# Planner of a fused attention, expert and MLP kernel: other lags, costs and engines in the plan, and the first expert's early rows split piece by piece

## The chip, the cores and the metric

One core of one Trainium2 chip. The time is that of one execution on the device in microseconds (us), the median of several runs. The engines are TensorE (PE in the rows, its weight loads PEld), VectorE (DVE), ScalarE (ACT), GpSimd (POOL) and SyncE (SP, which only starts transfers). They run side by side and wait for each other by semaphores.

## The reference, cut to what matters

```python
# q, k, v, alpha: [B=4, H=8, S=768, D=48]
for t in range(S):                                   # gated linear attention
    state = alpha[:, :, t, :, None] * state + einsum('bhd,bhe->bhde', k[:, :, t], v[:, :, t])
    y[:, :, t] = einsum('bhd,bhde->bhe', q[:, :, t], state)
x = y.transpose(0, 2, 1, 3).reshape(3072, 384)
logits = x @ w_gate                                  # [3072, 8]
expert_idx = argmax(logits, axis=1)                  # one expert for each token
gate_w = softmax(logits)[arange(N), expert_idx]
for e in range(8):                                   # w1: [8, 384, 1024], w2: [8, 1024, 384]
    xe = x[expert_idx == e]
    out[expert_idx == e] = gate_w[expert_idx == e, None] * (maximum(xe @ w1[e], 0) @ w2[e])
h = out @ w_in                                       # [3072, 384] @ [384, 2048]
return (h * (1 / (1 + exp(-1.702 * h)))) @ w_out     # @ [2048, 384]
```

## The kernel before, in words

**Attention.** The 3072 tokens are 24 tiles of 128 (`n` = 0 to 23; 4 batches of 6 chunks). For every group `g` of tiles VectorE forms running products of alpha by scans, forward (`Pf`, op `pf`) and backward (`Q`, op `qs`), and scales q with `Pf` (op `q`) and k with `Q` (op `k`). A scan of a group is cut into pieces of at most 386 columns; its second operand is a pattern of zeros and ones, `pat`. Op `k` runs on POOL for the groups in `MULT` (line 59), else on VectorE.

For each tile TensorE then forms scores (op `A`, into `atp`), ACT evicts them (`ats`), POOL masks them (an affine select), TensorE transposes k (op `K`, `ktp`), forms the product of k and v (`KV`, `kv`), the values (`X`, `xp` from `ats` and v) and the part from the state (`Y`, `xp` from q and `S`). The new state is the product plus the old state (op `SK`, an add on VectorE; for tiles with n < `ONTO`, line 60, TensorE adds the old state by a product with the identity instead) scaled on ACT. ACT evicts `x`, and TensorE forms `xtp` (op `T`), which holds the tile turned back and the eight logits.

**Routing**, for pairs of tiles (i = 0 to 11; 2i and 2i+1). VectorE: logits `lg`, their maximum, `d`, `sc`, `mx`, the one-hot choice `oh_all` (op `ch`, line 653) and running counts `cnt` (op `cn`). ACT: exponentials `ex`, their sum `gt` (VectorE inverts it) and the weighed rows `xw`, in four buffers, so that a pair's weighing needs the scatters of the pair two before. TensorE: op `B`, the rank (lines 683 to 688), three products that add into one PSUM tile:

```python
pe.matmul(ranks, ones, segr, start=True, stop=False)
pe.matmul(ranks, tri, oh_all[:, n0:n0 + 12, :], start=False, stop=False)
state["rk"] = pe.matmul(ranks, ones, cnt[:, n0:n0 + 12, :], start=False, stop=True)
```

VectorE makes row numbers `slots` of the ranks (op `so`), and POOL scatters the rows by them to `xs` in DRAM, sorted by expert (op `sc`, an indirect DMA). The ranks lie in the same PSUM tile as the scans' pattern (lines 379 to 381):

```python
bank = ps_1.tile([P, 512], F32, tag="lg", name="bank")
pat = bank[:, 0:HS]
ranks = bank[:, HS:HS + 12 * E].rearrange("p (n e) -> p n e", e=E)
```

**The plan.** All of this is handed to `Plan` (line 76) as ops: engine, cost in us, ops that it needs, a due time. `run` (line 124) simulates it 16 times: `passed` places, on the engine that can start first, the op with the smallest key among those that can start within `PATIENCE` of the earliest; an op is ready `HOP` after the ops that it needs; ops in `ALONE` on VectorE and POOL never overlap. Keys are due times first, then the latest starts of a pass backward from the end (the time after each op is the `tail` table), in the last 8 rounds with noise from `SEED`. The best order is then issued, and each engine keeps it. All these instructions carry line 73 (75 after).

**The end of the phase.** When 18 tiles are scattered, SP loads the first 224 rows of the first expert (op `early`, line 770). Behind T23, TensorE transposes them in three pieces of 128 columns each (op `te`, `turn_early`), and op `tx` splits them into a high and a low half, `xe_0` on ACT and `xe_1` on VectorE (`halve_early`). The first expert's first layer on these rows follows (line 331, `hp_0e` to `hp_7e`; ACT makes `he` of each), its second layer is line 348. On POOL pads follow the last scatters (line 812). Then the other rows, seven more experts (line 1005) and the second MLP.

Of the kernel before, what the change touches and what calls it, by code (L numbers as in the profile page):

```python
# [75 lines left out]
class Plan:  # L76
# [49 lines left out]
    def run(self, free, tail, rounds):  # L126
# [5 lines left out]
        self.apart = [name.rstrip("0123456789.") in ALONE.get(o[0], ()) for name, o in self.all.items()]  # L132
# [6 lines left out]
        rest = [tail.get(name, tail.get(name.rstrip("0123456789."), tail[""])) for name in names]  # L139
        hop = [HOP[e] for e in self.engine]  # L140
        rnd = random.Random(SEED)
        best = None
        for spread in (0.0, SPREAD):
            key = [o[3] for o in ops]
            for _ in range(rounds):
                start, order = self.passed(key, before, behind, lambda i, o: hop[i], ready, free)
# [11 lines left out]
def gla_moe_kernel(ctx: ExitStack, tc: tile.TileContext, hA, hkq, qT, kT, aT, qU, kU, aU, a0, v, wg, w1, w2, w_in, w_out, wgf, out):  # L158
# [198 lines left out]
    with ExitStack() as att:  # L357
# [196 lines left out]
        def step(n, got, pnds):
# [161 lines left out]
        for t, when in [("a.0", 4.1), ("k.0", 6.3), ("wg", 13.0)] + [(f"{t}.{c}", 7.0 + 3.2 * (c - 1) + w) for c in range(1, NC) for t, w in (("a", 0.6), ("k", 2.2))] + [(f"v{c}", 10.0 + 3.2 * c) for c in range(NC - 1)]:  # L716
# [665 lines left out]
```

## Time and profile before

| | us |
|---|---|
| median of 3 runs | 805.05 (804.11 to 806.07) |
| the profiled execution, by the clock of the runs | 804.12 |
| its span in the profile | 802.3 |
| mean granted clock of TensorE | 0.988 |
| attention and routing, up to the early rows' transposes | 0 to 143.6 |
| first expert's first product | 149.8 |
| experts and second MLP, TensorE busy throughout | to 790 |

The span is that of the records of one execution; the other 1.8 us lie around it. Times in rows are us from the span's start. A record's duration reaches a little into the next one's where instructions are pipelined. The bracket behind a row is the idle time of the engine before it and what ended it, as inferred from semaphores: with several semaphores the one that came last by the profile.

### The profile page before, as it was taken

Reading aid. Unit: us, or ns where it says so; the run is one execution under the profiler, and the core shown is the slowest. Engines: PE = TensorE matmul, PEld = TensorE weight load, DVE = VectorE, ACT = ScalarE, POOL = GpSimd, SP = SyncE. Lnnn points to the kernel's source line nnn. Section 1 sums busy time; section 2 is a strip of 40 time slices with the busy share of each in tenths; the row PEclk is TensorE's granted clock in tenths of the full one; section 3 lists DMA queues with packets and bytes.
Section 4 is the critical chain, followed back from the end, with each engine's and each line's share of the span. In section 5 each row is a group of like instructions: output and inputs, shape, how many; then the busy total and the mean of one; then the engine's idle time right before and its main releaser. Section 6 shows DMA issues by size and latency. Waiting matters only on the chain. (4 is left out here: it accounts for less than half of the span.)

```text
span 802.3 us, 13866 instructions
## 1 busy us (share of the span) xinstructions
PE 775.7 (97%) x5172; PEld 704.0 (88%) x5172; DVE 477.1 (59%) x913; ACT 382.4 (48%) x802; POOL 340.3 (42%) x435
## 2 busy tenths in 40 slices
PE   7998999799999999999999999999999999999995
PEld 5887778798889999999999989999999999999994
DVE  8988795569675657744588677754344443333331
ACT  5777787345463454445454455443333333223221
POOL 6663554509576658742366486550320303001001
PEclk9999999899999999999999999999999999999998
DMA  9998333357645564652134243220311303001001
GB/s 321 246 275 239 110 120 120 118 206 251 209 134 171 197 194 137 210 165 79 41 93 151 65 140 112 99 93 1 40 22 19 40 0 40 1 1 40 0 1 42
DMA packets 31836, 91.10 MB, mean 114 GB/s; under 512 B 6083, under 2 KB 11027, under 8 KB 31763
## 3 DMA queue, kind: packets, MB, share of 16 engines
q1 hardware_dynamic: 17584, 55.45, 22.7%
q0 software_dynamic: 11408, 30.98, 13.2%
q10 hardware_dynamic: 2771, 3.74, 1.5%
q8 instruction: 42, 0.69, 0.4%
q14 instruction: 31, 0.25, 0.1%
HBM read 70.87 MB, written 19.27 MB: 112 GB/s over the span
## 5 line engine op out<-in xcount | busy, mean ns | idle before, releaser
L1103 POOL DMA_INDIRECT out_y<-ob,perm x40 | 48.8, 1219 | 227.1 <-DVE ob L1099 216.9
L1069 DVE TENSOR_TENSOR h<-h,sg 128x512 f32<-128x512 f32 x96 | 66.9, 696 | 112.4 <-ACT sg L1068 112.1
L1088 PE MATMUL o<-whi,gh 128*128 128x384 f32 x384 | 130.1, 339 | 1.1 <-ACT gh L1072 1.1
L1088 PE MATMUL o<-wlo,gh 128*128 128x384 f32 x384 | 129.2, 337 | 0.0
L1088 PE MATMUL o<-whi,gl 128*128 128x384 f32 x384 | 126.2, 338 | 0.1
L1068 ACT ACTIVATE sg<-h 128x512 f32<-128x512 f32 x96 | 57.1, 595 | 118.5 <-PE h L1063 118.4
L1063 PE MATMUL h<-xh,wlo 128*128 128x512 f32 x288 | 113.2, 393 | 0.0
L1063 PE MATMUL h<-xh,whi 128*128 128x512 f32 x288 | 113.0, 392 | 0.0
L1063 PE MATMUL h<-xl,whi 128*128 128x512 f32 x288 | 112.6, 393 | 0.0
L1073 DVE TENSOR_TENSOR gl<-h,gh 128x512 fp32r<-128x512 f32 x96 | 66.3, 691 | 54.4 <-ACT gh L1072 52.7
L1072 ACT ACTIVATE gh<-h 128x512 fp32r<-128x512 f32 x96 | 57.4, 598 | 67.4 <-DVE h L1069 67.2
L1088 PEld LDWEIGHTS o<-whi,gh 128*128 128x128 f32 x384 | 72.1, 188 | 5.9 <-ACT gh L1072 1.9
L1088 PEld LDWEIGHTS o<-wlo,gh 128*128 128x128 f32 x384 | 72.1, 188 | 4.0
L1088 PEld LDWEIGHTS o<-whi,gl 128*128 128x128 f32 x384 | 71.8, 188 | 0.4 <-DVE gl L1073 0.4
L307 POOL TENSOR_TENSOR wlo<-stg,whi 128x512 fp32r<-128x512 f32 x42 | 57.6, 1398 | 18.8 <-ACT whi L299 18.7
L348 PE MATMUL yp<-hh,whi 128*128 128x224 f32 (+7 forms) x192 | 65.3, 343 | 0.2 <-ACT hh L333 0.2
L348 PE MATMUL yp<-hh,wlo 128*128 128x224 f32 (+7 forms) x192 | 64.9, 343 | 0.0
L1063 PEld LDWEIGHTS h<-xl,whi 128*128 128x128 f32 x288 | 54.1, 188 | 12.2
L348 PE MATMUL yp<-hl,whi 128*128 128x224 f32 (+7 forms) x192 | 63.2, 344 | 0.0
L1063 PEld LDWEIGHTS h<-xh,whi 128*128 128x128 f32 x288 | 54.2, 188 | 8.5
L1063 PEld LDWEIGHTS h<-xh,wlo 128*128 128x128 f32 x288 | 54.1, 188 | 8.4
L336 DVE SCALAR_TENSOR_TENSOR hl<-hp,hh 128x224 fp32r<-128x224 f32 (+7 forms) x64 | 34.8, 556 | 35.0 <-ACT hh L333 34.8
(269 smaller groups left out, 1574.6 us busy)
## 6 DMA issues: line engine op xcount, KB each, us to landing
stg<-in_w SPq DMA_DIRECT2D x30, 768.0 KB, 4.6
v<-in_v SPq DMA_DIRECT2D x24, 256.0 KB, 4.7
wf<-cvl POOLq DMA_DIRECT2D x48, 128.0 KB, 2.8
raw<-in_w_out POOLq DMA_DIRECT2D x24, 256.0 KB, 3.1
stg_m<-wf SPq DMA_DIRECT2D x8, 768.0 KB, 4.2
raw<-in_w_in POOLq DMA_DIRECT2D x18, 256.0 KB, 3.1
AB<-in_aU SPq DMA_DIRECT2D x24, 145.1 KB, 4.8
k<-in_kU SPq DMA_DIRECT2D x24, 144.0 KB, 4.6
```

Source lines behind the costliest of these rows:

```text
L307: POOL.tensor_sub(out=lo[:, cs], in0=st[:, cs], in1=hi[:, cs].bitcast(F32))
L336: DVE.scalar_tensor_tensor(out=h[1][:, f, :], in0=h_ps, scalar=0.0, in1=h[0][:, f, :].bitcast(F32), op0=ALU.max, op1=ALU.subtract)
L348: last["mm"] = PE.matmul(y_ps, w[:, c0:c0 + P], a[:, f, :], start=(i == 0), stop=(i == 23))
L1063: mm = PE.matmul(h_ps, w[:, c0:c0 + P], a[:, kk, :], start=(i == 0), stop=(i == 8))
L1068: ACT.activation(sg, h_ps, AF.Sigmoid, scale=QS)
L1069: DVE.tensor_mul(out=h_ps, in0=h_ps, in1=sg)
L1072: ACT.activation(gh, h_ps, AF.Copy)
L1073: DVE.tensor_sub(out=gl, in0=h_ps, in1=gh.bitcast(F32))
L1088: mm = PE.matmul(os[pt][t], a[:, ts], w[:, c0:c0 + DM], start=(f == f0 and first), stop=(f == f1 - 1 and a is gl))
L1103: POOL.indirect_dma_start(out=out_views[jj], out_offset=bass.IndirectOffsetOnAxis(ap=perm[:, jj:jj + 1], axis=0), in_=o_sb, in_offset=None ...
```

## The change

Costs in the plan are set nearer to what instructions take. A lag can now be set for a pair of ops: 2.5 us more from a scatter to what waits for it (a weighing, or the load of the early rows), 3.0 more from a pair's count to its rank, and 0.3 more into each op of TensorE from another engine. `PATIENCE`, `SEED`, the tail table and the load times are others. Four k products (groups 2, 7, 8 and 9) go from POOL to VectorE and two (10 and 16) from VectorE to POOL; the state of tile 4 is added on VectorE instead of TensorE. `te` and `tx` are cut into three ops each by 128 columns, with the low half (`tl`) an op of its own.

```diff
-MULT = (0, 1, 2, 3, 4, 5, 6, 7, 8, 9, 12)
-ONTO = 6
-SEED, SPREAD = 635, 0.6
-PATIENCE = {"PE": 0.03, "DVE": 0.05, "ACT": 0.3, "POOL": 0.3, "SP": 0.05}
+MULT = (0, 1, 3, 4, 5, 6, 10, 12, 16)
+ONTO = 4
+SEED, SPREAD = 582, 0.6
+PATIENCE = {"PE": 0.0, "DVE": 0.0, "ACT": 0.1, "POOL": 0.1, "SP": 0.1}
 ALONE = {"DVE": ("q", "k", "wl", "cn"), "POOL": ("s", "k", "pnd")}
+EXTRA = {("sc", "xw"): 2.5, ("sc", "early"): 2.5, ("cn", "B"): 3.0}
+EASE = 0.3
...
-        rest = [tail.get(name, tail.get(name.rstrip("0123456789."), tail[""])) for name in names]
-        hop = [HOP[e] for e in self.engine]
+        rest = [tail.get(name, tail.get(k, tail[""])) for name, k in zip(names, kind)]
+        lag = lambda i, o: HOP[self.engine[i]] + EXTRA.get((kind[i], kind[o]), EASE if self.engine[o] == "PE" != self.engine[i] else 0.0)
...
-                start, order = self.passed(key, before, behind, lambda i, o: hop[i], ready, free)
+                start, order = self.passed(key, before, behind, lag, ready, free)
...
-                late, _ = self.passed([-start[i] - self.cost[i] for i in every], behind, before, lambda i, o: hop[o], rest, dict.fromkeys(free, 0.0))
+                late, _ = self.passed([-start[i] - self.cost[i] for i in every], behind, before, lambda i, o: lag(o, i), rest, dict.fromkeys(free, 0.0))
...
-                    add(name, "POOL", 0.1 + 2.3 * f * part, [f"qs{g}", k_in], due - 0.6, lambda r=r: pool.tensor_mul(out=k[:, r], in0=ki[:, r], in1=it["Q"][:, r]))
+                    add(name, "POOL", 0.05 + 1.65 * f * part, [f"qs{g}", k_in], due - 0.6, lambda r=r: pool.tensor_mul(out=k[:, r], in0=ki[:, r], in1=it["Q"][:, r]))
...
-            add(f"q{g}", "DVE", 0.05 + 0.83 * f, [prev, q_in] + (ks if g == 0 else []), due, lambda: dve.tensor_mul(out=q, in0=qi, in1=it["Pf"][:, :, 0:CH]))
+            add(f"q{g}", "DVE", 0.05 + 0.83 * f, [prev, q_in], due, lambda: dve.tensor_mul(out=q, in0=qi, in1=it["Pf"][:, :, 0:CH]))
...
-            add(f"B{i}", "PE", 0.3, [f"cn{i}", f"so{i - 1}"], due + 14.5, rank)
+            add(f"B{i}", "PE", 0.28, [f"cn{i}", f"so{i - 1}"], due + 14.5, rank)
...
-                add(f"sc{n0 + j}", "POOL", 1.25, [f"so{i}", f"xw{n0 + j}"], due + 10 + 0.1 * j, lambda j=j: scatter(j))
...
+                add(f"sc{n0 + j}", "POOL", 1.1, [f"so{i}", f"xw{n0 + j}"], due + 10 + 0.1 * j, lambda j=j: scatter(j))
...
-        def turn_early():
-            xe.extend([ap.tile([P, KD, EARLY], F32R, name=f"xe_{i}") for i in range(2)])
-            for kk in range(KD):
-                turn_x0(pe, xe, 0, EARLY // GT, kk, ("kt", "kv", "at")[kk])
-
-        def halve_early():
-            for kk in range(KD):
-                halve_x0(act, dve, xe, 0, EARLY // GT, kk)
+        def turn_early(kk):
+            if kk == 0:
+                xe.extend(ap.tile([P, KD, EARLY], F32R, name=f"xe_{i}") for i in range(2))
+            turn_x0(pe, xe, 0, EARLY // GT, kk, ("kt", "kv", "at")[kk])
+
+        def high_early(kk):
+            last["x0"] = act.activation(xe[0][:, kk, :], state["t0", 0, kk], AF.Copy)
+
+        def low_early(kk):
+            last["lo"] = dve.tensor_sub(out=xe[1][:, kk, :], in0=state["t0", 0, kk], in1=xe[0][:, kk, :].bitcast(F32))
 
         plan.need("wh3", f"x{NT - 1}")
         plan.need("wl3", "unused")
-        add("te", "PE", 2.4, ["early", f"T{NT - 1}"], BEGIN + PITCH * (NT + 1), turn_early)
-        add("tx", "ACT", 1.1, ["te"], BEGIN + PITCH * (NT + 2), halve_early)
-        plan.run({"DVE": 4.0, "ACT": 4.0, "POOL": 5.3, "PE": 6.3, "SP": 14.0}, {f"T{NT - 1}": 29.0, f"sc{NT - 1}": 25.0, "wl2": 25.0, "wl3": 21.0, "jk": 0.0, "qm": 0.0, "": 19.0}, 8)
+        free = ["early", f"T{NT - 1}", f"KV{NT - 2}", f"x{NT - 1}"]
+        for kk in range(KD):
+            add(f"te{kk}", "PE", 0.8, free, BEGIN + PITCH * (NT + 1) + kk, lambda kk=kk: turn_early(kk))
+            add(f"tx{kk}", "ACT", 0.33, [f"te{kk}"], BEGIN + PITCH * (NT + 1) + kk, lambda kk=kk: high_early(kk))
+            add(f"tl{kk}", "DVE", 0.33, [f"tx{kk}"], BEGIN + PITCH * (NT + 1) + kk, lambda kk=kk: low_early(kk))
+        plan.run({"DVE": 3.9, "ACT": 4.0, "POOL": 5.3, "PE": 6.3, "SP": 14.0}, {"te": 25.0, "tx": 25.0, "tl": 25.0, "B": 23.0, "sc": 19.0, "unused": 18.5, "wl3": 19.0, "wl2": 22.0, "jk": 0.0, "qm": 0.0, "": 19.0}, 8)
```

Other lines of the diff set costs alone, as `rec` 0.17 to 0.14, `s` 0.8 to 0.64 or `gt` 0.2 to 0.13.

How the order moves. On VectorE, around the second piece of the scan Q16, where the choice (`mx14`, `oh_all`) and the count (`cnt`) of tiles 14 and 15 and the slots of pair 6 (`so12`) stand, before:

```order
L73 SCALAR_TENSOR_TENSOR sc14_1788<-d14_1786,desc8_76 128x16
L73 TENSOR_REDUCE mx14_1790<-sc14_1788 128x2
L73 TENSOR_TENSOR oh_all_102<-desc8_76,mx14_1790 128x16
L73 SCALAR_TENSOR_TENSOR Q16_1800<-AB_158,bank_155 128x386
L73 RECIPROCAL AB_158<-Pf17_1732 128x6
L73 SCALAR_TENSOR_TENSOR Q16_1800<-AB_158,bank_155 128x386
L73 TENSOR_TENSOR cnt_150<-cnt_150,oh_all_102 128x8 x2
L73 RECIPROCAL gt14_1832<-gt14_1832 128x2
L73 TENSOR_TENSOR k_0_157<-k_0_157,Q16_1800 128x768
```

and after:

```order
L75 TENSOR_REDUCE mx14_1793<-sc14_1791 128x2
L75 TENSOR_TENSOR oh_all_102<-desc8_76,mx14_1793 128x16
L75 TENSOR_TENSOR q_0_156<-q_0_156,Pf16_1661 128x768
L75 TENSOR_TENSOR cnt_150<-cnt_150,oh_all_102 128x8 x2
L75 SCALAR_TENSOR_TENSOR Q16_1769<-AB_158,bank_155 128x386
L75 RECIPROCAL gt14_1826<-gt14_1826 128x2
L75 TENSOR_TENSOR so12_1840<-bank_155,oh_all_102 128x16
L75 TENSOR_REDUCE slots_103<-so12_1840 128x2
L75 SCALAR_TENSOR_TENSOR Q17_1846<-AB_158,bank_155 128x386
L75 TENSOR_TENSOR q_0_156<-q_0_156,Pf17_1730 128x768
```

The count of tiles 14 and 15 has come ahead of the second piece of Q16, with the product q16 ahead of both, and the slots of pair 6, which need its rank, have come right behind that piece. Before, they stood behind the first piece of Q17.

On TensorE, around the rank of pair 6 (the three products into `bank`; xp16 and xp17 are the outputs of tiles 16 and 17, atp18 and atp19 scores, xtp14 and xtp15 op T), before:

```order
L73 MATMUL xp16_1716<-ats16_1_1638,v_4_139 64x128
L73 LDWEIGHTS ones_72
L73 MATMUL bank_155<-segr_151,ones_72 128x96
L73 LDWEIGHTS tri_74
L73 MATMUL bank_155<-oh_all_102,tri_74 128x96
L73 LDWEIGHTS ones_72
L73 MATMUL bank_155<-cnt_150,ones_72 128x96
L73 MATMUL xtp14_1743<-wsel_147,x14_1611 128x104 x4
L73 MATMUL xtp15_1752<-wsel_147,x15_1696 128x104 x4
L73 MATMUL xp16_1716<-q_0_156,S15_1656 48x128 x8
L73 MATMUL atp18_0_1774<-q_0_156,k_0_157 128x128
```

and after:

```order
L75 MATMUL xp17_1804<-ats17_1_1741,v_5_140 64x128
L75 LDWEIGHTS ones_72
L75 MATMUL bank_155<-segr_151,ones_72 128x96
L75 LDWEIGHTS tri_74
L75 MATMUL bank_155<-oh_all_102,tri_74 128x96
L75 LDWEIGHTS ones_72
L75 MATMUL bank_155<-cnt_150,ones_72 128x96
L75 MATMUL xp17_1804<-q_0_156,S16_1754 48x128 x8
L75 MATMUL kv18_1848<-v_0_135,kts18_1819 64x48 x8
L75 MATMUL atp19_0_1860<-q_0_156,k_0_157 128x128
```

The rank has moved from the middle of tile 16's output to the middle of tile 17's.

On ACT, at the end of the phase (`xe_0` are the high halves of the early rows, `xw22` the weighed rows of the last pair, `ex22` and `gt22` its exponentials and sums, `he_q` the first expert's), before:

```order
L73 ACTIVATE x23_2307<-xp23_2258 128x512
L299 ACTIVATE whi3_2310<-AB_158 128x1536
L73 ACTIVATE ex22_2344,ss22_2345<-d22_2335 128x8 x2
L73 ACTIVATE gt22_2348<-ss22_2345 128x2
L73 ACTIVATE xw22_1_2354<-xtp23_2313,gt22_2348 128x384
L73 ACTIVATE xw22_0_2359<-xtp22_2302,gt22_2348 128x384
L73 ACTIVATE xe_0_2322<-tp0_0_0_2324 128x224
L73 ACTIVATE xe_0_2322<-tp0_1_0_2327 128x224
L73 ACTIVATE xe_0_2322<-tp0_2_0_2330 128x224
L333 ACTIVATE he_q_0_2390<-hp0_0e_2431 128x224
```

and after:

```order
L75 ACTIVATE x23_2302<-xp23_2272 128x512
L302 ACTIVATE whi3_2304<-AB_158 128x1536
L75 ACTIVATE xe_0_2322<-tp0_0_0_2324 128x224
L75 ACTIVATE ex22_2343,ss22_2344<-d22_2329 128x8 x2
L75 ACTIVATE xe_0_2322<-tp0_1_0_2337 128x224
L75 ACTIVATE gt22_2352<-ss22_2344 128x2
L75 ACTIVATE xe_0_2322<-tp0_2_0_2347 128x224
L75 ACTIVATE xw22_0_2357<-xtp22_2297,gt22_2352 128x384
L75 ACTIVATE xw22_1_2360<-xtp23_2312,gt22_2352 128x384
L336 ACTIVATE he_q_0_2391<-hp0_0e_2432 128x224
```

The three splits have come ahead of both weighings, with the exponentials and the sum between them.

## Rows read from the trace of the kernel before

**Rows 1.** page, section 1: busy us (share of the span) xinstructions
```profile
PE 775.7 (97%) x5172; PEld 704.0 (88%) x5172; DVE 477.1 (59%) x913; ACT 382.4 (48%) x802; POOL 340.3 (42%) x435
```

**Rows 2.** windows: stretch, length, busy (x) by engine, clock, DMA, GB/s
```profile
12.50:118.50 106.00, 99.78 (x1374) 85.91 (x1373) 94.28 (x205) 82.98 (x248) 59.88 (x79) 0.97 0.75 212
...
155.00:790.00 635.00, 632.49 (x3373) 583.31 (x3373) 349.67 (x590) 268.99 (x477) 251.30 (x281) 1.00 0.31 95
```

**Rows 3.** timeline of PE, the ranks: start, us, operation [idle before <-releaser]
```profile
46.59 0.20 PE L73 MATMUL bank<-oh_all,tri 128*128 128x96 bf16 x1 [0.63 <-DVE oh_all L73]
...
65.11 0.20 PE L73 MATMUL bank<-segr,ones 128*128 128x96 bf16 x1 [2.19 <-DVE gt L73]
...
86.55 0.20 PE L73 MATMUL bank<-oh_all,tri 128*128 128x96 bf16 x1 [1.85 <-DVE oh_all L73]
...
105.00 0.20 PE L73 MATMUL bank<-segr,ones 128*128 128x96 bf16 x1 [0.89 <-DVE Pf L73]
...
120.28 0.20 PE L73 MATMUL bank<-oh_all,tri 128*128 128x96 bf16 x1 [0.97 <-ACT ex L73]
```

**Rows 4.** windows, the stretches in which the granted clock was low
```profile
66.30:70.00 3.70, 3.70 (x28) 3.25 (x28) 2.74 (x4) 2.48 (x5) 1.22 (x3) 0.57 0.93 250
...
86.70:91.40 4.70, 4.70 (x50) 3.93 (x48) 3.94 (x9) 2.08 (x6) 0.60 (x2) 0.64 0.19 56
...
149.70:155.00 5.30, 5.24 (x24) 5.24 (x25) 4.26 (x14) 1.22 (x5) 4.08 (x5) 0.50 0.31 113
```

**Rows 5.** timeline of PE, from the last count to the first expert
```profile
145.45 0.20 PE L73 MATMUL bank<-cnt,ones 128*128 128x96 bf16 x1 [0.21 <-DVE cnt L73]
...
149.76 1.05 PE L331 MATMUL hp_0e<-xe,whi 128*128 128x224 f32 x3 [4.11 <-ACT xe L73]
```

**Rows 6.** timeline of DVE, scans beside a rank
```profile
63.84 0.35 DVE L73 TENSOR_TENSOR SK<-kv,S 128x192 f32<-128x192 f32 x1
...
64.11 0.95 DVE L73 TENSOR_TENSOR_SCAN Q<-AB,bank 128x386 f32<-128x386 f32 x1
...
105.33 0.96 DVE L73 TENSOR_TENSOR_SCAN Pf<-AB,bank 128x386 f32<-128x386 f32 x1 [0.38 <-PE bank L73]
```

**Rows 7.** groups of DVE, 12.5 to 118.5: busy, mean ns | idle before
```profile
L73 DVE TENSOR_TENSOR k<-k,Q 128x768 f32<-128x768 f32 x7 | 7.2, 1034 | 0.0
...
L73 DVE TENSOR_TENSOR SK<-kv,S 128x192 f32<-128x192 f32 x8 | 2.8, 355 | 3.7 <-PE kv L73 3.1 <-ACT ats L73 0.6
...
L73 DVE TENSOR_REDUCE lg<-xtp 128x8 f32<-128x32 f32 x18 | 3.2, 180 | 2.4 <-PE xtp L73 2.4
...
L73 DVE TENSOR_TENSOR cnt<-cnt,oh_all 128x8 bf16<-128x8 bf16 x16 | 5.0, 316 | 0.8 <-PE bank L73 0.5
...
L73 DVE TENSOR_TENSOR d<-lg,m 128x16 f32<-128x16 f32 x8 | 4.8, 601 | 0.3
```

**Rows 8.** timeline of PE and DVE, around A18 and at the early transposes
```profile
108.06 0.49 PE L73 MATMUL atp<-q,k 64*128 64x128 f32 x4
...
109.58 0.92 DVE L73 TENSOR_TENSOR_SCAN Q<-AB,bank 128x386 f32<-128x386 f32 x1
...
143.56 0.26 PE L73 MATMUL tp<-ident,AB 112*128 112x112 f32 x1
```

**Rows 9.** timeline of POOL and DVE, a held subtraction
```profile
83.00 1.68 POOL L73 TENSOR_TENSOR k<-k,Q 128x768 f32<-128x768 f32 x1
...
84.63 1.21 POOL L73 TENSOR_SCALAR_AFFINE_SELECT ats<-ats 128x512 f32<-128x512 f32 x2
...
83.64 2.24 DVE L73 TENSOR_TENSOR d<-lg,m 128x16 f32<-128x16 f32 x1
```

**Rows 10.** timeline of POOL and ACT, ahead of the first expert
```profile
146.28 0.97 POOL L73 DMA_INDIRECT xs<-xw,slots  x1 [0.30 <-DVE room L474]
...
148.88 0.58 ACT L73 ACTIVATE xw<-xtp,gt 128x384 f32<-128x384 f32 x1 [0.61 <-DMA xs<-xw,slots]
...
149.36 0.84 ACT L73 ACTIVATE xe<-tp 128x224 fp32r<-128x224 f32 x3
```

More of the change, by code (lines that the diff above doesn't have):

```diff
@@ L131, in run @@
         self.engine, self.cost = [o[0] for o in ops], [o[1] for o in ops]
-        self.apart = [name.rstrip("0123456789.") in ALONE.get(o[0], ()) for name, o in self.all.items()]
+        kind = [name.rstrip("0123456789.") for name in names]
+        self.apart = [k in ALONE.get(o[0], ()) for k, o in zip(kind, ops)]
         before = [[at[t] for t in o[2] if t in at] for o in ops]
@@ L533, in prep @@
             for h0 in range(0, w, HS):
-                prev = add(f"pf{g}.{h0}", "DVE", 0.05 + 0.9 * min(HS, w - h0) / HS, [a_in, prev] + [f"{t}{g - 2}" for t in ("q", "qm", "pnd")], due - 3.6 * f - 6.4, lambda h0=h0: pf(h0))
-            add(f"rec{g}", "DVE", 0.17, [prev], due - 2.9 * f - 6.3, lambda: dve.reciprocal(out=blocks(AB[:, o:o + w])[:, :, CH], in_=it["Pf"][:, :, CH - 1]))
-            add(f"qm{g}", "ACT", 0.15, [prev], due + 9, lambda: act.activation(qmin[:, b * NP + p:b * NP + p + m, c0:c1], it["Pe"], AF.Square))
+                prev = add(f"pf{g}.{h0}", "DVE", 0.02 + 0.85 * min(HS, w - h0) / HS, [a_in, prev] + [f"{t}{g - 2}" for t in ("q", "qm", "pnd")], due - 3.6 * f - 6.4, lambda h0=h0: pf(h0))
+            add(f"rec{g}", "DVE", 0.14, [prev], due - 2.9 * f - 6.3, lambda: dve.reciprocal(out=blocks(AB[:, o:o + w])[:, :, CH], in_=it["Pf"][:, :, CH - 1]))
+            add(f"qm{g}", "ACT", 0.11, [prev], due + 9, lambda: act.activation(qmin[:, b * NP + p:b * NP + p + m, c0:c1], it["Pe"], AF.Square))
             if c2 > c0:
@@ L542, in prep @@
             for h0 in range(0, w, HS):
-                qs = add(f"qs{g}.{h0}" if h0 + HS < w else f"qs{g}", "DVE", 0.05 + 0.9 * min(HS, w - h0) / HS, [qs, f"jk{g - 2}"] + [f"{t}{g - 2}.{i}" for t in ("k",) for i in range(NP)], due - 2.7 * f - 0.2, lambda h0=h0: back(h0))
+                qs = add(f"qs{g}.{h0}" if h0 + HS < w else f"qs{g}", "DVE", 0.02 + 0.85 * min(HS, w - h0) / HS, [qs, f"jk{g - 2}"] + [f"{t}{g - 2}.{i}" for t in ("k",) for i in range(NP)], due - 2.7 * f - 0.2, lambda h0=h0: back(h0))
             add(f"jk{g}", "ACT", 0.15 + 0.85 * f, [f"qs{g}"], due + 10, bound)
@@ L630, in step @@
                 add(f"a{j}.{n}", "ACT", 0.5, [f"A{n}", f"X{n - 2}"], at + 2 + 0.1 * j, lambda j=j: evict(j))
-                add(f"s{j}.{n}", "POOL", 0.8, [f"a{j}.{n}"], at - 3 + 0.1 * j, lambda j=j: pool.affine_select(out=it[j], in_=it[j], pattern=[[0, NP], [1, CH]], compare_op=ALU.is_ge, fill=0.0, base=0, channel_multiplier=-1))
+                add(f"s{j}.{n}", "POOL", 0.64, [f"a{j}.{n}"], at - 3 + 0.1 * j, lambda j=j: pool.affine_select(out=it[j], in_=it[j], pattern=[[0, NP], [1, CH]], compare_op=ALU.is_ge, fill=0.0, base=0, channel_multiplier=-1))
             if c < NC - 1:
@@ L644, in step @@
             add(f"T{n}", "PE", 1.0, [f"x{n}", "wsel", f"xw{n - 2}", f"lg{n - 2}"], now + PITCH + 4.2, project)
-            add(f"lg{n}", "DVE", 0.17, [f"T{n}", f"ch{i - 2}"], now + 2 * PITCH + 3.5, logits)
+            add(f"lg{n}", "DVE", 0.14, [f"T{n}", f"ch{i - 2}"], now + 2 * PITCH + 3.5, logits)
         def pair(i):
@@ L703, in pair @@
             add(f"cn{i}", "DVE", 0.3, [f"ch{i}"], due + 3, count)
-            add(f"ex{i}", "ACT", 0.55, [f"ch{i}"], due - 5, sums)
-            add(f"gt{i}", "ACT", 0.2, [f"ex{i}"], due + 1.2, gate)
+            add(f"ex{i}", "ACT", 0.52, [f"ch{i}"], due - 5, sums)
+            add(f"gt{i}", "ACT", 0.13, [f"ex{i}"], due + 1.2, gate)
             add(f"gr{i}", "DVE", 0.1, [f"gt{i}"], due - 18.6, lambda: dve.reciprocal(out=it["gt"], in_=it["gt"]))
@@ L713, in pair @@
             for j in range(G):
[L714 to L716 removed]
+                add(f"sc{n0 + j}", "POOL", 1.1, [f"so{i}", f"xw{n0 + j}"], due + 10 + 0.1 * j, lambda j=j: scatter(j))
+        for t, when in [("a.0", 3.9), ("k.0", 6.3), ("wg", 12.0)] + [(f"{t}.{c}", 6.8 + 2.9 * (c - 1) + w) for c in range(1, NC) for t, w in (("a", 0.0), ("k", 1.4))] + [(f"v{c}", 9.2 + 2.9 * c) for c in range(NC - 1)]:
             plan.given(t, when)
```

## The prediction, made before the changed kernel ran

> **What bounds the kernel now.** I read the page's busy shares first (TensorE 97% [rows 1]), then the windows of each stage [rows 2]. From 155 to 790 us TensorE is busy 632.49 of 635 us at full clock: the experts and the second MLP leave nothing, and the change does not touch them. All that can move lies in the first 155 us. There TensorE is busy 99.78 of 106 us and VectorE 94.28 of 106 [rows 2], so neither has much room, and what decides is who waits for whom in the planned order.
>
> The timeline of TensorE shows it. The three products of a pair's rank (into `bank`) are where it waits: 0.63, 2.19, 1.85, 0.89 and 0.97 us [rows 3], 6.53 in sum. The clock table [rows 4] shows a second price: after the 2.19 wait the granted clock was 0.57 for 3.70 us, after the 1.85 wait 0.64 for 4.70 us, after the 4.11 wait before the first expert [rows 5] 0.50 for 5.30 us. The lower level is 1.2 GHz instead of 2.4, so these cost 3.70 x 0.43 = 1.6, 4.70 x 0.36 = 1.7 and 5.30 x 0.50 = 2.65 us. After the waits of 0.89 and 0.97 no such stretch follows.
>
> Why ranks wait has two answers. The releasers `oh_all` (three times, once under the name of `ex`, which follows the same chain) say that the choose chain came late: 0.63 + 1.85 + 0.97 = 3.45 us. The other two are scans: `bank` holds both the pattern that every scan reads and the ranks, so a rank's first product waits for the last scan planned ahead of it. A Q scan begun at 64.11 ends at 65.06 and the rank starts at 65.11 [rows 3, 6]; the row names `gt`, but that had long been done. It also works the other way round: a scan at 105.33 waited 0.38 us for the rank [rows 6].
>
> **The change, part by part.** *Slack before ranks* (cn to B 3.0, PE 0.3 extra). Ranks are planned later, and I expect the three waits on `oh_all`, 3.45 us, to go, with the 1.7 us of clock behind the second. The scan lock is not in the planner's list. In the changed order the rank of pair 6 stands in X17 instead of X16, and its first product will wait for the second piece of Q16, which has its slots right behind it; I count four ranks (pairs 2, 3, 5, 6) with a scan just ahead, where before there were two. So a wait on a scan is what is late next, and VectorE's progress sets the end.
>
> *Work on VectorE.* Up to the second Q16 scan, the one that the rank of pair 6 will wait for, the order of after adds k7, k8 and k9 (1.03 each [rows 7]), k2 (four of six chunks, two thirds of that, 0.69), q16 (the same shape and operation as a k, 1.03), one SK add (0.36 [rows 7]) and two counts (0.32 each [rows 7]), and takes away k10 (1.03): 3.09 + 0.69 + 1.03 + 0.36 + 0.64 - 1.03 = 4.8. Rows overlap: an add of 0.35 begun at 63.84 ends after 64.11, where the scan starts [rows 6], so some 0.08 of each of these instructions goes, and about as much again by the counts, whose mean of 0.32 holds some that were held: +3.8 us, with bounds of 3.0 and 4.8. Against that stand VectorE's own idle times of 106.00 - 94.28 = 11.72 us [rows 2]: 3.1 in front of SK adds and 2.4 in front of logits are ended by TensorE [rows 7], 5.5 together. They mirror the waits that the new slack removes, so I take these 5.5 as recovered and the other 6.2 as staying. Before, that Q16 scan ended at 109.58 + 0.92 = 110.50 [rows 8]. After: 110.5 + 3.8 - 5.5 = 108.8. With nothing recovered 114.3; with 9 of the 11.7 recovered and 3.0 added 104.5.
>
> *The rest of the main phase.* Before, TensorE had from A18 at 108.06 to the early transposes at 143.56 [rows 8] 35.50 us of work, 0.97 of it the wait at 120.28. In the new order A18, K18 and X17's first half stand ahead of the rank of pair 6, 20 products at 0.12 by the row of A18 (0.49 for four), 2.45; and one rank less has been done, +0.3. Left: 35.50 - 0.97 - 2.45 + 0.3 = 32.4. Rank at 108.8 + 0.1, transposes at 141.3, gain 2.25; I keep 0.25 back for other hops: **2.0 us**. TensorE's own work would allow the rank at 108.06 + 2.45 - 5.56 (the first four waits) - 3.3 (clock) - 0.5 (the identity product of kv4, dropped by ONTO, taken as four products of A18's size) = 101.2, so VectorE is the bound by 7 us; that the clock loss and the dropped product return is hidden behind it. Range for this term: -3.6 (nothing recovered) to +7.
>
> *Moves on POOL* (k2, k7 to k9 away, k10 and k16 there) have no price on the path by themselves, with POOL busy 59.88 of 106 us [rows 2]. What they cost is a hold: VectorE's `d`, 128x16, took 2.24 us at 83.64 while POOL did a k (83.00) and two masks (to 85.8) [rows 9]. The eight `d` took 4.8 us [rows 7], the other seven so 0.37 each: 1.9 us of hold in this one, which goes if that k no longer runs there. I cost the moves at nothing, with bounds of -1.9 and +4.9 (four moved products, each held by a pair of masks, 1.21 [rows 9]).
>
> The Trainium skill, "SBUF — State Buffer", section "Who interferes with whom", says that a VectorE instruction with two SBUF inputs contends with a GpSimd instruction that reads SBUF, and that whoever issues first keeps the shared ports for the whole instruction. The 2.24 us row agrees. It speaks against this change, since four two-input products go to VectorE; by it the sum would lose up to those 4.9 us.
>
> *Early rows, split one by one.* Before, all three transposes, then all three splits, and on ACT the splits stand behind ex22, gt22 and both weighings. The second weighing ends its wait for a scatter at 148.88 and the splits come at 149.36 [rows 10], so the first expert product starts at 149.76 after 4.11 us of wait [rows 5], 6.20 us after 143.56. In the new order on ACT stand xe 0, ex22, xe 1, gt22, xe 2 and only then the weighings. None of them waits for a scatter. The first product then needs two transposes (0.26 each [rows 8]), one split (0.28, a third of 0.84 [rows 10]) and two hops, about 1 us; but rank products of the last pair stand among the first products, and their count was ready at 145.45 [rows 5], 1.9 us after 143.56. So 2.0 instead of 6.2: 4.2 gained. Two things give back some: scatters and pads now follow beside the first expert, 1.27 apart (0.97 and the 0.30 ahead of it [rows 10]), so later transposes can wait, and VectorE's low halves stand among the unused-rows chain; the rows price neither, I bound both together by 0 and 1.3 and take 0.8. **3.4 us** (2.9 to 4.2). Whether the early rows land in time I take as before, at no price.
>
> *Clock.* Without the 4.11 wait I expect no half-clock stretch from 149.7 to 155: 2.65 by [rows 4], **2.5** taken, for part of it may come back after a 2 us pause (bound 0: after 1.85 us it fell as well).
>
> Sum: 2.0 + 3.4 + 2.5 = 7.9. The profiled execution took 804.12 (span 802.3 and 1.8 around it); 804.12 - 7.9 = 796.2. It was 0.9 below the median of 805.05, so on the scale of the medians **797.1 us**.
>
> **Rivals.**
> - *All waits go.* VectorE keeps up, scans are never late: 6.53 + 3.3 of clock + 0.5 for kv4 = 10.3, and 5.9 at the early rows: 16.2, 788.9. For it: 11.7 us of idle on VectorE, of which nobody knows how much returns. Against: four ranks adjacent to scans and 3.8 us more work.
> - *VectorE recovers nothing.* Q16 ends at 114.3, transposes at 146.9, 3.3 lost; early rows still give 5.9, perhaps 1.6 lost to one more half-clock stretch: 802.5 to 804. For it: the idle ended by TensorE may only turn into idle ended by POOL or ACT.
> - *The wait moves behind the first products.* The early rows land as late as before, or ACT's weighings hold up `he` for the second product; the pause returns there with the clock: the early part gives 2 and the main part 2: 801.
> - *Slower: the scan lock.* The moved products are held by mask pairs (+4.9) with nothing recovered: the Q16 scan ends at 110.5 + 3.8 + 4.9 = 119.2, transposes at 151.7, 8.1 lost, and 1.7 of clock at a longer wait, against 5.9: +3.9, 809. It decides from the point where that scan ends later than about 118.
>
> **How the numbers follow.** Forecast 0.52 (its own range 793 to 800), all waits go 0.12, nothing recovered 0.17, moved wait 0.11, scan lock 0.08. This measurement can tell about 0.2% from no change, 803.4 to 806.7. Faster: 0.52 + 0.12 + 0.11 and half of 0.17, in sum 0.83; same: the other half, 0.08; slower 0.09. The range leaves out the last rival and most of the first: 790 to 803.5.
>
> **What would show it.** Right: on ACT the three xe splits before the weighings, the first expert product within 2.5 us of the transposes, a granted clock near 1.00 over the 5 us behind it; no wait on `oh_all` at ranks, a wait on a scan at the ranks of pairs 2, 3, 5 or 6; the second Q16 scan ending near 109 and the transposes starting near 141.5. Wrong: that scan beyond 114, or an equal pause in front of the second expert product (the chain would name a scatter there), or half-clock stretches at new places.

## The result, and the profile after

The changed kernel takes 791.48 us (median of 4 runs, 789.69 to 792.89) against 804.62 (4 runs, 804.11 to 806.07): a ratio of 0.983, interval 0.981 to 0.986, or 13.1 us. The prediction was 797.1 (790.0 to 803.5). The profiled execution took 792.1 (span 790.1), 12.0 less than that of before. Where it went, by the starts of the same instructions on TensorE in the two profiles:

| | before | after | gained so far |
|---|---|---|---|
| early rows' transposes | 143.56 | 135.14 | 8.42 |
| first product of the first expert | 149.76 | 135.95 | 13.81 |
| its third hidden product | 155.09 | 139.86 | 15.23 |
| a later expert's product (in both it waits 1.08 us for `hl`) | 196.29 | 184.89 | 11.40 |
| span | 802.3 | 790.1 | 12.2 |

So the phase before the early rows gave 8.4 us, the early rows 6.8, and 3.8 went back between 140 and 185 us. The time lies in the stated range, but outside the forecast's own 793 to 800: it came between that and the rival that all waits go (788.9).

The ranks with a wait, on TensorE's timeline after (start, us, operation, [idle before <-releaser]); they answer to [rows 3]:

```profile
60.67 0.20 PE L75 MATMUL bank<-segr,ones 128*128 128x96 bf16 x1 [0.58 <-DVE Q L75]
...
71.16 0.20 PE L75 MATMUL bank<-segr,ones 128*128 128x96 bf16 x1 [0.76 <-DVE gt L75]
...
92.58 0.20 PE L75 MATMUL bank<-segr,ones 128*128 128x96 bf16 x1 [0.32 <-DVE Pf L75]
...
102.53 0.20 PE L75 MATMUL bank<-segr,ones 128*128 128x96 bf16 x1 [0.22 <-DVE Q L75]
```

These are pairs 2, 3, 5 and 6, the four with a scan just ahead: 1.88 us instead of 6.53 for all. Of the waits on `oh_all` in the main phase one of 0.16 us is left (at 130.64), and the slow clock there is gone, as the windows show (length, busy us of PE, PEld, DVE, ACT and POOL, granted clock, DMA share, GB/s; they answer to [rows 2, 4]):

```profile
12.50:118.50 106.00, 103.43 (x1459) 88.98 (x1458) 97.70 (x224) 89.13 (x269) 59.49 (x81) 1.00 0.81 225
12.50:102.50 90.00, 87.46 (x1235) 75.11 (x1234) 86.02 (x200) 74.61 (x230) 49.30 (x70) 1.00 0.87 235
151.90:156.00 4.10, 4.03 (x23) 4.06 (x24) 0.69 (x2) 0.81 (x3) 0.73 (x2) 0.60 0.97 313
```

The second row ends with the second piece of Q16, which before ended at 110.5. In between VectorE is busy 86.02 us and idle 3.98. Its groups after, from 12.5 to 118.5 (count | busy us, mean ns | idle before), answer to [rows 7]:

```profile
L75 DVE TENSOR_TENSOR k<-k,Q 128x768 f32<-128x768 f32 x8 | 8.1, 1006 | 0.0
L75 DVE TENSOR_TENSOR SK<-kv,S 128x192 f32<-128x192 f32 x11 | 3.8, 346 | 1.9 <-PE kv L75 1.9
L75 DVE TENSOR_TENSOR d<-lg,m 128x16 f32<-128x16 f32 x9 | 3.8, 417 | 0.3
...
L75 DVE SCALAR_TENSOR_TENSOR sc<-d,desc 128x16 f32<-128x16 f32 x9 | 3.3, 370 | 0.3
L75 DVE TENSOR_TENSOR cnt<-cnt,oh_all 128x8 bf16<-128x8 bf16 x18 | 2.9, 163 | 0.5 <-PE bank L75 0.2
```

A count takes 163 ns instead of 316, a `d` 417 instead of 601: the same instructions, less often held. In [rows 9] such a hold of a `d` lay beside work of POOL. The `sc` behind a `d` took 175 ns before (8 of them, 1.4 us) and takes 370 now, so a part of the holds has only moved.

The end of the phase, on TensorE (answers to [rows 5, 8]), on ACT [rows 10], and on VectorE and POOL:

```profile
135.14 0.74 PE L75 MATMUL tp<-ident,AB 112*128 112x112 f32 x6
...
135.95 0.37 PE L334 MATMUL hp_0e<-xe,whi 128*128 128x224 f32 x1
...
151.97 0.42 PE L781 MATMUL tp<-ident,AB 112*128 112x112 f32 x1 [2.46 <-DMA AB<-xs]
```

```profile
135.54 0.36 ACT L75 ACTIVATE xe<-tp 128x224 fp32r<-128x224 f32 x1
...
136.71 0.34 ACT L75 ACTIVATE xe<-tp 128x224 fp32r<-128x224 f32 x1
137.67 1.05 ACT L75 ACTIVATE xw<-xtp,gt 128x384 f32<-128x384 f32 x2 [0.61 <-DVE gt L75]
```

```profile
143.00 0.17 DVE L492 TENSOR_SCALAR psl<-room 128x2 int32<-128x2 f32 x1
143.08 1.75 DVE L312 TENSOR_TENSOR wlo<-AB,whi 128x1536 fp32r<-128x1536 f32 x1
```

```profile
143.45 2.23 POOL L821 DMA_INDIRECT xs<-zt,psl  x1 [2.10 <-DVE psl L492]
145.98 0.97 POOL L821 DMA_INDIRECT xs<-zt,psl  x1 [0.30 <-issue]
```

The first expert starts 0.81 us behind the transposes, before any weighing. It then runs into something new: the load of the other rows (`AB<-xs`) lands at 151.9, since it follows the two pads, the pads follow their row numbers (`psl`, 143.00), and the first pad takes 2.23 us, the second 0.97; beside the first VectorE splits a weight. TensorE waits 2.46 us and then runs at a granted clock of 0.60 for 4.10 us.

### The profile page after: what moved, and what is told of

It is laid out like the page before. It is cut to its first block, busy times and chain, and to the rows that moved or that the text cites. A ratio compares the mean times of both kernels' runs of the same rounds, so it can differ in the third digit from the quotient of the medians.

```text
span 790.1 us, 13882 instructions
## 1 busy us (share of the span) xinstructions
PE 771.9 (98%) x5170; PEld 700.4 (89%) x5170; DVE 473.2 (60%) x916; ACT 381.5 (48%) x802; POOL 336.7 (43%) x433
## 5 line engine op out<-in xcount | busy, mean ns | idle before, releaser
L1071 PEld LDWEIGHTS h<-xl,whi 128*128 128x128 f32 x288 | 54.1, 188 | 12.2
```

Of the source, the lines that this page charges most:

```text
L1071: mm = PE.matmul(h_ps, w[:, c0:c0 + P], a[:, kk, :], start=(i == 0), stop=(i == 8))
```

## The experiments

In some of them the plan's order is fixed: the list that the planner found is written into the kernel and edited, so that nothing else moves. A ratio is that to before, measured beside the kernel in question.

```diff
-        for i in best[1]:
+        for i in [at[name] for name in ORDER]:
```

**The early rows alone.** Two kernels, each with the other's order at the end of the phase (of the lists only the transposes, ACT's ops and the low halves; the ops between them are left out):

```diff
 # after:  T23 te0 te1 tx0 ex11 te2 tl0 tx1 gt11 tl1 tx2 xw22 tl2 xw23 ...
 # before: T23 te ex11 gt11 xw23 xw22 tx ...
```

After with the end of before. 

> The order of after up to T23, but the early rows transposed and split as before (three transposes, then both weighings, then three splits on ACT). Theory A (what follows the early rows sets the end: ranks, pads, load of the other rows, whose landing TensorE now meets at 151.97 with 2.46 us of wait): the first product comes 3 to 4 us later and 2.6 us of clock are lost there, but 3 to 4 us of the later wait and its slow clock go, so only 2 to 4 us are lost: 793.5 to 795.5. Rival B (the split is worth its full term): 5.4 us and 2.65 of clock lost, 799 or more.

Before with the end of after. 

> The order of before up to T23, with the early rows split one by one as in after. Theory A: the first product comes some 5 us earlier at full clock, but the pads and the load of the other rows land when they did (load issued at 157.4), so TensorE waits 3 to 5 us in front of their transposes: 801 to 803.5, 1 to 3.5 us faster than before. Rival B: the full 5.4 + 2.65: 797.

Measured: 794.42 us (ratio to before 0.985, 0.982 to 0.989) and 805.01 (1.000, 0.997 to 1.002). TensorE's waits in the first and in the second:

```profile
138.57 0.87 PE L334 MATMUL hp_0e<-xe,whi 128*128 128x224 f32 x3 [1.25 <-ACT xe L75]
...
141.27 1.15 PE L334 MATMUL hp_0e<-xe,whi 128*128 128x224 f32 x3 [1.50 <-DVE xe L75]
```

```profile
170.00 0.32 PE L778 MATMUL tp<-ident,AB 112*128 112x112 f32 x1 [3.45 <-DMA AB<-xs]
```

Theory A's range holds for the first: without the split 2.9 us are lost, not 8, and the wait for the other rows is gone. The second misses it (801 to 803.5): nothing is gained. Its profile is of a longer execution (810.26 us) than the median, so its rows are read from its transposes on: a later expert's product follows 53.85 us behind them (149.20 to 203.05), in before 52.73. The split wins time ahead of the load of the other rows, and this load does not land when it did, as theory A had it, but later:

| | early transposes | `psl` | load issued by SP |
|---|---|---|---|
| before | 143.56 | +5.54 | +13.87 |
| before with the end of after | 149.20 | +11.28 | +18.46 |
| after with the end of before | 135.24 | +5.51 | +10.72 |
| after | 135.14 | +7.86 | +14.44 |

The rows of the first three kernels, and the load of after:

```profile
149.10 0.17 DVE L489 TENSOR_SCALAR psl<-room 128x2 int32<-128x2 f32 x1
...
157.43 0.78 SPq L179 DMA_DIRECT2D AB<-xs  x2
```

```profile
155.64 0.39 DVE L336 SCALAR_TENSOR_TENSOR he_k<-hp_0e,he_q 128x224 fp32r<-128x224 f32 x1 [1.65 <-ACT he_q L333]
...
159.97 0.39 DVE L336 SCALAR_TENSOR_TENSOR he_k<-hp_2e,he_q 128x224 fp32r<-128x224 f32 x1 [2.09 <-ACT he_q L333]
...
160.48 0.17 DVE L489 TENSOR_SCALAR psl<-room 128x2 int32<-128x2 f32 x1
...
167.66 0.78 SPq L179 DMA_DIRECT2D AB<-xs  x2
```

```profile
140.75 0.39 DVE L492 TENSOR_SCALAR psl<-room 128x2 int32<-128x2 f32 x1
...
145.96 0.78 SPq L182 DMA_DIRECT2D AB<-xs  x2
```

```profile
149.58 0.78 SPq L182 DMA_DIRECT2D AB<-xs  x2
```

With the new end the first products come so early that the low halves of their hidden layer (`he_k`) stand among VectorE's steps towards `psl`, and there VectorE waits for ACT. With the old end these steps run through first. So the split puts the load off by 3.7 to 4.6 us against the transposes, and TensorE waits for it. `psl` itself comes 5.7 and 2.4 us later; why the time from `psl` to the load differs (5.2 to 8.3 us in the table) is not shown.

**The load taken out of the way.** The transposes of the other rows go behind the eighth hidden product:

```diff
-        transpose_x0(xr, EARLY // GT, NG, ("xt", "lt", "at"))
+        with tc.issue_after(last["h7"].ins): transpose_x0(xr, EARLY // GT, NG, ("xt", "lt", "at"))
```

> After, with the other rows' first transposes put behind the eighth first-layer product of the early rows, instead of ahead of it. Theory A (the load of the other rows lands at 151.9 and TensorE meets it 2.46 us too soon, with 1.6 us of slow clock behind): 2.9 us of products now lie in front of the wait, it goes and the clock stays: 3 to 4 us faster, 787.5 to 788.5. Rival: the landing does not bound, the wait only moves behind: 790 to 792.

And with the pads sooner, `he_k` from the third on behind `psl`:

```diff
-            DVE.scalar_tensor_tensor(out=h[1][:, f, :], ...
+            with tc.issue_after(last["psl"].ins) if tag and f >= 2 else ExitStack(): DVE.scalar_tensor_tensor(out=h[1][:, f, :], ...
```

> As the one before, and the low halves of the early rows' hidden layer from the third on put behind the row numbers of the pads on VectorE, so that the pads start 1 to 2 us sooner (psl at 142.2 instead of 143.0). Theory A: once the transposes stand behind the eighth product nothing is left to wait for: within 0.5 us of that kernel. Rival: if that kernel still shows a wait for the load, this one takes 1 to 2 us of it.

Measured: 787.31 (0.980, 0.977 to 0.983) and 787.34 (0.981, 0.978 to 0.984). In the first the transposes start without a wait, and the clock stays at 1.00:

```profile
150.53 0.53 PE L781 MATMUL tp<-ident,AB 112*128 112x112 f32 x2
```

```profile
150.00:156.00 6.00, 6.00 (x56) 5.85 (x55) 3.98 (x16) 2.91 (x9) 0.97 (x2) 1.00 0.98 330
```

Theory A's range holds twice. 791.48 - 787.31 = 4.2 us; the wait and the clock were 2.46 + 4.10 x 0.40 = 4.1. Both kernels beat before and after. The second says little: its pads hardly came sooner (`psl` 6.61 us behind the early transposes instead of 6.86, the load 13.68 instead of 13.67). The version with the old end (794.42) waits for no load either and is 7.1 us behind 787.31; in the two profiles 1.0 of that lies ahead of the early transposes, where the orders are the same, and 5.9 behind them (to the same later product 187.07 - 135.24 = 51.83 and 180.19 - 134.26 = 45.93). So I take the split to be worth some 6 us once the load no longer bounds; the old end with the transposes moved was not run.

**The engine of the k products**, in a fixed order.

```diff
-MULT = (0, 1, 3, 4, 5, 6, 10, 12, 16)
+MULT = (0, 1, 2, 3, 4, 5, 6, 7, 8, 9, 12)
```

Above, in the order of after. 

> The order of after, but the k products on the engines of before: k2, k7, k8, k9 back on POOL, k10 and k16 back on VectorE, each at its place in the order. Theory C (k on POOL holds VectorE's small operations of the routing chain, so that counts and choices come late): cnt and d grow by 3 us in sum, waits at ranks return, 4 to 7 us slower than after: 795.5 to 798.5. Rival D (the slack in front of the ranks removed the waits, and it does not matter which engine has these k): within 1.5 us of after, or faster for 2.7 us less of work on VectorE.

The other way round, in the order of before. 

> The order of before, but the k products on the engines of after: k2, k7, k8, k9 on VectorE, k10 and k16 on POOL. Theory C: the held counts (mean 316 ns) fall towards 160, the waits of 2.19 and 1.85 in front of ranks shrink and with them the slow clock: 3 to 6 us faster than before, 799 to 802. Rival D: no gain from it without slack; 2.7 us more of work on VectorE make it 0 to 4 us slower, 805 to 809.

Measured: 794.41 (0.986, 0.983 to 0.989) and 805.16 (1.000, 0.998 to 1.002). Counts in the first and in the second (window 3 to 120):

```profile
L75 DVE TENSOR_TENSOR cnt<-cnt,oh_all 128x8 bf16<-128x8 bf16 x18 | 3.0, 169 | 0.3
```

```profile
L73 DVE TENSOR_TENSOR cnt<-cnt,oh_all 128x8 bf16<-128x8 bf16 x16 | 5.6, 347 | 0.8 <-PE bank L73 0.5
```

Theory C's cause falls: with k back on POOL counts stay short, with k on VectorE they stay long. But the first time lies in neither range. Its transposes come at 137.50, 2.4 later than in after, with one wait of 1.70 at the rank of pair 2 where after had 0.58: in the order of after the choice of engines is worth 2.9 us by the medians, through that wait and not through held counts. In the second profile the wait of 2.19 is down to 0.56, with the clock at 1.00 behind it, as theory C said, but the time did not change.

**Slack alone, and after without it.**

```diff
+EXTRA = {("cn", "B"): 3.0}                         # in before
-EXTRA = {("sc", "xw"): 2.5, ("sc", "early"): 2.5, ("cn", "B"): 3.0}
-EASE = 0.3
+EXTRA = {("sc", "xw"): 2.5, ("sc", "early"): 2.5}  # in after
+EASE = 0.0
```

> Before with one line more: 3.0 us from a pair's count to its rank in the plan, which is then made again; costs, engines, seed and early rows as in before. Theory S: the waits on oh_all (0.63, 1.85, 0.97) go and half of the waits on scans, 4 to 7 us faster: 798 to 801. Rival P: the order gets no better by more than 2 us, since the rest of the plan still takes wrong costs: 803 to 807.

> After with the plan made again without the slack in front of ranks (no 3.0 from a count to its rank, no 0.3 into TensorE); costs, engines, seed and early rows as in after. Theory S (the slack is what removed the waits at ranks): TensorE again waits 3 to 5 us in sum for oh_all, the clock falls once or twice: 796 to 800. Rival P (the costs nearer to the trace and the other engines made the better order, the slack adds little): within 2 us of after, 790 to 794.

Measured: 798.03 (0.994, 0.992 to 0.996) and 796.34 (0.992, 0.989 to 0.994). Theory S, by the times of both. Before with slack starts the transposes at 137.56 instead of 143.56; one wait of 2.33 us on a scan is left at a rank (41.04). After without slack has long waits again, one on a scan and one on `oh_all`, and a `d` that is held:

```profile
82.93 0.20 PE L75 MATMUL bank<-segr,ones 128*128 128x96 bf16 x1 [2.63 <-DVE Pf L75]
...
105.30 0.20 PE L75 MATMUL bank<-oh_all,tri 128*128 128x96 bf16 x1 [2.56 <-DVE oh_all L75]
```

```profile
L75 DVE TENSOR_TENSOR d<-lg,m 128x16 f32<-128x16 f32 x9 | 6.5, 726 | 0.3
L75 DVE TENSOR_TENSOR cnt<-cnt,oh_all 128x8 bf16<-128x8 bf16 x18 | 2.8, 154 | 0.3
```

But its transposes still come at 139.60, 4.0 sooner than before. The counts are short here too, without slack, so something else shortens them; the next run tries the costs.

**The costs on POOL alone.**

```diff
-add(name, "POOL", 0.1 + 2.3 * f * part, ...
+add(name, "POOL", 0.05 + 1.65 * f * part, ...
-add(f"s{j}.{n}", "POOL", 0.8, ...
+add(f"s{j}.{n}", "POOL", 0.64, ...
-add(f"sc{n0 + j}", "POOL", 1.25, ...
+add(f"sc{n0 + j}", "POOL", 1.1, ...
```

> Before with three costs on POOL set as in after (k 0.1 + 2.3 f to 0.05 + 1.65 f, a mask 0.8 to 0.64, a scatter 1.25 to 1.1), the plan made again; no slack, the engines of k and the early rows as before. Theory K (with true costs the plan's rule that counts and POOL's masks and k do not overlap holds on the chip): counts fall from a mean of 0.31 us towards 0.16, and 1 to 4 us are gained, 800 to 803. Rival (the holds and waits go with the slack alone): counts stay above 0.25 and the time within 1.5 us of before.

Measured: 798.95 (0.993, 0.991 to 0.995), 5.6 us below the 804.51 of before beside it; counts and `d`:

```profile
L73 DVE TENSOR_TENSOR cnt<-cnt,oh_all 128x8 bf16<-128x8 bf16 x18 | 3.2, 176 | 0.7 <-PE bank L73 0.4
L73 DVE TENSOR_TENSOR d<-lg,m 128x16 f32<-128x16 f32 x9 | 3.0, 337 | 0.3
```

Counts fall as theory K said, and the gain is more than it expected (1 to 4 us). The plan keeps counts apart from masks and k on POOL (`ALONE`), and with costs near the trace the counts are no longer held; `d` belongs to an op (`ch`) that is not in `ALONE`, so why it got shorter is not shown. Without any slack no rank waits for `oh_all` here; one waits for a scan:

```profile
51.21 0.20 PE L73 MATMUL bank<-segr,ones 128*128 128x96 bf16 x1 [1.41 <-DVE Pf L73]
```

So slack by itself and costs by themselves both take these waits away, and after without slack, which has the costs, has one of 2.56. Each of these kernels has a plan made again, and another order alone may win or lose some us: before planned again with neither edit (another seed, say) was not run.

**Slack and the engines of k** in before, the order that of slack alone.

```diff
+EXTRA = {("cn", "B"): 3.0}
-MULT = (0, 1, 2, 3, 4, 5, 6, 7, 8, 9, 12)
+MULT = (0, 1, 3, 4, 5, 6, 10, 12, 16)
```

> Before with the 3.0 us from count to rank (798.03 by itself), its plan's order kept, and the k products on the engines of after. Theory C (k on POOL holds the routing chain, which shows once the ranks have slack): 1.5 to 3 us faster than with slack alone, 795 to 796.5. Rival D (VectorE only gets 2.7 us more work): 798 to 801.

Measured: 796.72 (0.990, 0.986 to 0.994), between the two ranges; the ratio overlaps with that of slack alone. The profile speaks against theory C: counts 378 ns, transposes at 139.65, 2.1 later than with slack alone (some 1.65 of it a stretch at a clock of 0.67 from 40 to 45 us). The time cannot show this loss, since in both kernels TensorE then waits for the load of the other rows, which lands at the same time although `psl` is 2.1 us apart (147.76 and 149.86; why is not shown); slack alone first, then with the engines of k:

```profile
157.81 0.32 PE L780 MATMUL tp<-ident,AB 112*128 112x112 f32 x1 [2.48 <-DMA AB<-xs]
```

```profile
157.80 0.32 PE L780 MATMUL tp<-ident,AB 112*128 112x112 f32 x1 [0.38 <-DMA AB<-xs]
```

A later expert's product starts at 189.26 in both. So 798.03 too holds a wait for the load, and what slack gives in the main phase is more than its time says.

**The seed.**

```diff
-SEED, SPREAD = 582, 0.6
+SEED, SPREAD = 635, 0.6
```

> After with the seed of before, the plan made again: how much of the gain is this one draw. Theory S (slack, costs and engines carry it): within 2 us of 791.5. Rival (the draw is a good part of it): 794 to 799.

Measured: 791.09 (0.983, 0.978 to 0.987). The plan came out the same, instruction for instruction, so this is a second measurement of after and says nothing on draws.

**The pattern apart from the ranks**, from the version of 787.31:

```diff
-        pat = bank[:, 0:HS]
+        pat = ap.tile([P, HS], F32, name="pat")
```

> The version with the other rows' transposes behind the eighth product, and the scans' pattern in an SBUF tile of its own instead of the ranks' PSUM bank, so that no rank waits for a scan and no scan for a rank. Theory L (the bank is what ties them): the waits of 0.87, 0.39, 0.22 and 0.21 in front of ranks go, 1.5 us faster: 785.8 to 786.5. Rival (the scans now read two SBUF operands, and by the Trainium skill, "SBUF — State Buffer", section "Who interferes with whom", such an instruction contends with POOL's reads): the scans' mean grows from 0.94 us, and with 58 of them on an engine that is busy 92% the main phase gets 3 to 10 us longer, 790 to 797.

Measured: 802.63 (0.998, 0.995 to 1.000), 15 us slower than without the edit. No rank waits for a scan any more, but the scans and POOL's masks (3 to 140 us) are longer:

```profile
L75 DVE TENSOR_TENSOR_SCAN Q<-AB,pat 128x386 f32<-128x386 f32 x30 | 38.6, 1289 | 0.3
L75 DVE TENSOR_TENSOR_SCAN Pf<-AB,pat 128x386 f32<-128x386 f32 x30 | 31.4, 1054 | 1.5 <-DMA AB<-in_hA 1.5
```

```profile
L75 POOL TENSOR_SCALAR_AFFINE_SELECT ats<-ats 128x512 f32<-128x512 f32 x46 | 39.4, 872 | 20.9 <-ACT ats L75 20.6
```

Without the edit they take 944, 940 and 693 ns. The rival's mechanism holds, at more than its price: 30 scans x 0.345 and 30 x 0.114 are 13.8 of the 15 us. The bank that ties ranks to scans costs 1.7 us of waits without the edit, far less than scans with both operands in SBUF beside POOL.

## Why the prediction came out as it did

*Waits at ranks.* Right: those on `oh_all` went but for 0.16 us, waits on scans stayed at the ranks of pairs 2, 3, 5 and 6. The clock came back with them.

*VectorE as the bound* is the step that failed: "After: 110.5 + 3.8 - 5.5 = 108.8", and "VectorE is the bound by 7 us". The scan ended at 102.47 and the rank of pair 6 started at 102.53, 1.3 us behind the 101.2 that TensorE's own work allowed by the prediction's sum. VectorE in the window that ended with the same scan before, and its counts and `d` there and in after's window:

```profile
12.50:110.50 98.00, 91.78 (x1256) 78.83 (x1257) 86.97 (x193) 75.58 (x228) 54.99 (x74) 0.97 0.77 216
```

```profile
L73 DVE TENSOR_TENSOR cnt<-cnt,oh_all 128x8 bf16<-128x8 bf16 x15 | 4.9, 326 | 0.8 <-PE bank L73 0.5
L73 DVE TENSOR_TENSOR d<-lg,m 128x16 f32<-128x16 f32 x8 | 4.8, 601 | 0.3
```

```profile
L75 DVE TENSOR_TENSOR d<-lg,m 128x16 f32<-128x16 f32 x8 | 3.5, 437 | 0.3
...
L75 DVE TENSOR_TENSOR cnt<-cnt,oh_all 128x8 bf16<-128x8 bf16 x16 | 2.4, 151 | 0.3
```

Idle then 98.00 - 86.97 = 11.03 us, after 3.98: 7.05 recovered, 5.5 predicted, which is near. The 3.8 us of added work were not: VectorE was busy 0.95 us less. The products were added (3.6 us more of k and q), but counts and `d` lost as much in holds (2.5 and 1.3). The prediction had "I cost the moves at nothing" with a bound of -1.9, looked for the cause in the engine of k, and left the plan's own costs without any price. Three of them by themselves are worth 5.6 us, slack by itself 5.9 to 6.6 us against the two medians of before, the engines of k 2.9 in the order of after. These overlap, and no run parts them further. `PATIENCE`, the tail table, the load times, `ONTO` and the lag behind a scatter were not tried alone.

With VectorE no longer in the way, what TensorE itself lost came back, from 12.5 to the early transposes, before and after:

```profile
12.50:143.56 131.06, 123.84 (x1703) 106.44 (x1702) 107.49 (x252) 103.33 (x303) 70.27 (x91) 0.97 0.67 194
```

```profile
12.50:135.14 122.64, 119.73 (x1682) 102.89 (x1681) 104.06 (x254) 101.59 (x301) 66.55 (x90) 1.00 0.74 209
```

TensorE is idle 2.91 us instead of 7.22 and busy 4.1 us less; 3.3 of these 4.1 are the clock that the prediction priced and held to be hidden behind VectorE. What followed the anchor was right: 32.6 us from that rank to the transposes, 32.4 predicted. So the main phase gave 8.4, not 2.0, and the scan and the transposes missed the marks that were set for being right (109 and 141.5) on the fast side.

*Early rows.* The mechanism was right, and so were its two first terms together: up to the third hidden product they gave 6.8 us, 4.2 and 2.5 predicted. Singly they were not: 5.4 to the first product, since the rank of the last pair came behind it and not ahead, and 1.4 of clock from there. The give-back was mis-sized: "I bound both together by 0 and 1.3 and take 0.8", where it was 2.46 of wait and 1.64 of clock, 4.1. The prediction saw that pads and loads follow beside the first expert and that low halves stand among VectorE's chain, but priced one pad's pitch, not the chain from the last rank to the landing, which the split itself puts off. The slow stretch at a new place, one of its signs of being wrong, came. From the transposes to that later expert's product 2.98 us came (52.73 to 49.75), 5.9 predicted.

So 2.0 + 5.9 stood against 8.4 + 3.0: two errors of opposite sign. That the sum came as near as it did is luck. Of the rivals, "all waits go" (10.3 in the main phase) was nearer for the first part, and "the wait moves behind the first products" for the second, though at a load and not at ACT. The scan lock is real and small.

*The Trainium skill*, "SBUF — State Buffer", "Who interferes with whom": the pattern's run agrees with it (backward scans 944 ns with the second operand in PSUM, 1289 from SBUF). The page gives "for the whole instruction" in its point on VectorE's two-port modes; for a two-input instruction the 2.24 us row is what shows a hold that long. Its cost for the moved products did not show: the k products on VectorE took 1006 ns, 1034 before.

## What to carry to other kernels

A planner's costs are worth measuring: with three of them near the trace, a rule that keeps two engines from holding each other showed on the chip (counts 316 to 176 ns). Lags in front of the engine that must not wait paid as well. Before a stall is credited as a gain, look what lands next: work that moves up without its transfers waits for them, and can put them off; the whole chain in front of a transfer (row numbers, pads, load) is the price, not its last link. Where two kernels wait for the same load, their times do not compare what lies ahead of it. Two errors that cancel look like a good forecast; compare stage by stage.

## What the runs showed of the hardware that was not expected

A scan of 386 columns took 944 ns (backward) or 940 (forward) with its second operand in PSUM and 1289 or 1054 with it in SBUF beside a busy POOL, and POOL's masks grew from 693 to 872.

The length of a wait did not by itself say whether TensorE's clock fell behind it. It fell after 1.85 us (0.64), 2.19 (0.57, both in before) and 2.46 (0.60, after). It stayed at 1.00 after 2.33 (41 to 46 us) and 2.48 (157.8 to 162) with slack alone, and after 2.63 in after without slack (82.9 to 88).

The start of before varies. In three profiles with its order up to there (one with k2 on VectorE) the first scan starts at 3.90, 4.28 and 4.35 us, and the first `xtp` at 17.92, 20.14 and 21.89: 0.45 us late become 4.0. In the latter two a forward scan then waits 1.29 and 2.23 us for POOL, where masks stand ahead. That the late first scan is the cause is not shown. In after the first scan started at 4.13 and `xtp` at 18.65. All runs of before lie between 801.2 and 809.7, those of after and of its repeat between 789.7 and 792.9.
